# Routed experts behind attention and a dense feed-forward: expert weights split by two engines instead of three, a third early block, and three smaller moves

## Chip, cores and metric

One core of one Trainium2 chip. The metric is device microseconds (us) of one execution; lower is better. Before the change the median of 3 runs is 950.04 us (948.1 to 950.38).

## The reference

Three stages follow one another on 4608 tokens (8 batches of 576) of 512 values.

```python
# attention in chunks of 64, 8 heads of 64
scores = scale * q_c @ k_c.T ; attn = softmax(scores) ; x = attn @ v_c      # 4608 x 512
# dense feed-forward, d_ff 768
h = np.maximum(np.maximum(x @ w1, x @ w2), x @ w3)
x = h @ w_out
# routed experts: only tokens with a positive skip score, one of 8 experts each
do_compute = x @ w_skip > 0
e_idx = np.argmax(xc @ w_gate, axis=1) ; gate_w = softmax(xc @ w_gate)[e_idx]
out[do_compute] = xc + gate_w * (np.maximum(xc @ w1[e], 0) @ w2[e])         # w1 512x1024, w2 1024x512
```

With the inputs that the reference draws, its own routing sends 404, 159, 28, 89, 123, 65, 3 and 85 rows to the experts 0 to 7; of them 318, 105, 21, 70, 109, 25, 0 and 53 come from the first 4096 tokens.

## The kernel before

All stages share one program whose order on every engine is written out by hand, so an instruction that waits holds back all that is behind it on its engine. Every product is made from two halves: a weight or an activation is split into hi (rounded) and lo (the rest), and three matmuls (hi x hi, hi x lo, lo x hi) are summed.

Tokens go through attention and feed-forward in 9 chunks of 512 (`i` = 0 to 8, 8 is `LAST`). While chunk `i` is in the feed-forward, which has 18 slots (6 columns `f` of 128, times 3 weight matrices `m`), attention of the next tokens runs between its matmuls, VectorE makes the routing scores of the chunk before, and chunk `i-2` is placed in the experts' table: `route_pick` in slot 0, `route_place` in slot 2. `route_place` counts with two small matmuls (L532, L533) into a PSUM tile `pos`, which VectorE reads at L537 and L539; `pos` takes its turn in the PSUM ring of the tag "S", from which attention's transposes (`PT`, L279) take theirs too. At a column's end `ff_lo` (L347) makes the lo half of the hidden values on GpSimd, for the very last column on VectorE.

After the last chunk four output tiles are finished (`out_tile`, matmuls at L358). Among them TensorE transposes rows for the routing scores (`logits_turn`, L472, then `logits_pe`, L479) and the rows of two early blocks (`block_x`, L614). `logits_turn(2)` and `block_x` share one PSUM tile, `pxt[0]`.

Then come the experts. A block takes 128 rows of one expert: `block` has 12 matmuls (`first`, L634) for each half of the hidden values, ReLU on ScalarE (L639), four transposes (`turn`, L643) whose hi goes to ScalarE (L645) and lo to VectorE (L646), and 24 matmuls `second` (L651) whose sum VectorE scales by the gate and adds to the rows (L674); GpSimd scatters the rows back to `out` with an indirect DMA (L679). A block's rows come by an indirect DMA from `out` on GpSimd's queue (`gather`, L606), and `block_x` transposes them. Expert 0's first two blocks can start before the routing is complete, since their rows are old ones, of the first 4096 tokens. After them the kernel gathers for all experts from the complete table (`inf_e`, L889; index arithmetic L926 and L927), and every expert has one block whose place is fixed and further blocks behind branches on its count (`chain`, L986).

An expert's weights come in 8 pieces of 512 KB through a ring of 8 raw buffers, loaded on SyncE's queue (`expert_load`, L580 and L584), and `expert_split` makes hi and lo of each while the block of the expert before it runs. Five pieces have hi on ScalarE (L600) and lo on VectorE (L601); the pieces 0, 3 and 6 (for expert 0 two, for expert 1 one) have hi on VectorE (L597) and lo on GpSimd (L598):

```python
if n == 0 or n == 3 and e != 1 or n == 6 and e > 1:
    nc.vector.tensor_copy(hi, t)                                             # L597
    nc.gpsimd.tensor_tensor(out=lo, in0=t, in1=hi.bitcast(F32), op=ALU.subtract)
else:
    nc.scalar.activation(hi, t, AF.Copy)                                     # L600
    nc.vector.tensor_tensor(out=lo, in0=t, in1=hi.bitcast(F32), op=ALU.subtract)
```

## Time and profile before

| | |
|---|---|
| runs, median (lowest to highest) | 950.04 us (948.1 to 950.38) |
| the profiled execution | 951.15 us, its span 949.3 us |
| mean granted TensorE clock | 0.973 of full speed |
| busy: TensorE | 886.6 us, 93% of the span |
| busy: VectorE, ScalarE, GpSimd | 653.4, 286.3, 280.1 us |
| HBM | 80.27 MB read, 12.93 MB written |

The profile names the engines PE (TensorE), PEld (its weight loads), DVE (VectorE), ACT (ScalarE), POOL (GpSimd) and SP (SyncE); a q behind the name is the engine's queue of instructions. Times of single rows count from the start of the span. The routed experts' blocks lie from about 757 to 943 us. The fixed block of expert 1 starts at 821.70, its second at 834.6, then one block each of the experts 2 to 7 begins at 851.2, 866.7, 881.1, 895.3, 910.1 and 928.0. In a timeline row "x4" stands for four instructions in a row, and the bracket tells how long the engine had been idle and what it had waited for.

### The profile page before, as it was taken

The numbers are of one execution on the slowest core, as the hardware profiler recorded it, in microseconds if no ns is written. First come the engines' busy times: TensorE is split into PE (matmuls) and PEld (weight loads), VectorE is DVE, ScalarE is ACT, GpSimd is POOL, SyncE is SP. The second block draws the span as 40 slices with busy tenths as digits, with TensorE's granted clock in tenths as the row PEclk, the third lists the DMA queues.
The fourth block names the chain that finished last, engine by engine and source line by source line (L and its number), as shares of the span: only waits on it lengthen the run. The fifth ranks groups of instructions, "written<-read, shape, count | busy, mean of one in ns | idle before, by whom it ended". The sixth has DMA issues, their size and how long they took to land. (4 is left out here: it accounts for less than half of the span.)

```text
span 949.3 us, 16425 instructions
## 1 busy us (share of the span) xinstructions
PE 886.6 (93%) x6048; PEld 730.0 (77%) x6048; DVE 653.4 (69%) x1374; ACT 286.3 (30%) x468; POOL 280.1 (30%) x204
## 2 busy tenths in 40 slices
PE   7599999999999999999999999999999896989886
PEld 6597778887887887888788788788887775768664
DVE  4668945987777787687787777677582371458983
ACT  4466532112112122112221222221211441335451
POOL 2258841113102111111211211221125132345772
PEclk8799999999999999999999999999999997989999
DMA  7766762224123123212412413100600544146870
GB/s 171 187 161 162 195 196 41 58 49 97 33 51 79 34 37 90 54 30 56 83 30 38 102 32 59 51 7 1 222 1 23 177 129 147 58 157 221 291 258 11
DMA packets 215361, 92.04 MB, mean 97 GB/s; under 512 B 187015, under 2 KB 196487, under 8 KB 215122
## 3 DMA queue, kind: packets, MB, share of 16 engines
q1 hardware_dynamic: 212098, 86.67, 34.7%
q0 software_dynamic: 3152, 3.95, 1.3%
q8 instruction: 63, 1.03, 0.5%
q14 instruction: 48, 0.39, 0.1%
HBM read 80.27 MB, written 12.93 MB: 98 GB/s over the span
## 5 line engine op out<-in xcount | busy, mean ns | idle before, releaser
L331 PE MATMUL A<-arena 128*128 128x512 f32 (+1 forms) x2016 | 471.2, 388 | 1.6 <-POOL arena L404 1.2
L331 PEld LDWEIGHTS A<-arena 128*128 128x128 f32 x2016 | 365.6, 189 | 75.8 <-POOL arena L404 2.6
L466 DVE CUSTOM_DVE_ANT_0 junk<-x,wb 128x512 bf16<-128x512 f32 x270 | 209.6, 776 | 5.9
L347 POOL TENSOR_TENSOR arena<-hs,arena 128x512 fp32r<-128x512 f32 x53 | 80.8, 1524 | 438.4 <-ACT arena L343 438.3
L358 PE MATMUL X<-arena 128*128 128x512 f32 x648 | 158.4, 393 | 1.8 <-POOL arena L347 1.8
L340 DVE TENSOR_TENSOR hs<-A,hs 128x512 f32<-128x512 f32 x108 | 74.2, 687 | 121.4 <-PE A L331 120.5
L358 PEld LDWEIGHTS X<-arena 128*128 128x128 f32 x648 | 122.1, 190 | 27.9 <-POOL arena L347 2.2
L343 ACT ACTIVATE arena<-hs 128x512 fp32r<-128x512 f32 x54 | 34.1, 631 | 239.4 <-DVE hs L340 239.4
L634 PE MATMUL pa<-arena,xT 128*128 128x512 f32 x288 | 79.3, 426 | 7.8 <-PEq L986 3.8
L601 DVE TENSOR_TENSOR arena<-ew,arena 128x1024 fp32r<-128x1024 f32 x43 | 62.7, 1481 | 19.9 <-ACT arena L600 19.9
L634 PEld LDWEIGHTS pa<-arena,xT 128*128 128x128 f32 x288 | 56.4, 203 | 24.3 <-issue 9.1
L651 PE MATMUL py<-arena 128*128 128x512 f32 x288 | 72.0, 397 | 1.4 <-DVE arena L646 1.3
L598 POOL TENSOR_TENSOR arena<-ew,arena 128x1024 fp32r<-128x1024 f32 x21 | 59.5, 2839 | 28.4 <-DVE arena L597 8.8
L651 PEld LDWEIGHTS py<-arena 128*128 128x128 f32 x288 | 53.0, 189 | 14.1 <-DVE arena L646 2.4
L556 POOL DMA_INDIRECT tab<-inf,idx x36 | 39.7, 1103 | 75.6 <-DMA tab<-inf,idx 46.3
L258 DVE TENSOR_REDUCE mx<-S 128x8 f32<-128x512 f32 x36 | 24.8, 690 | 44.5 <-PE S L247 44.5
L338 ACT ACTIVATE hs<-A 128x512 f32<-128x512 f32 x54 | 32.2, 596 | 71.8 <-PE A L331 59.3
L600 ACT ACTIVATE arena<-ew 128x1024 fp32r<-128x1024 f32 x43 | 43.8, 1058 | 21.6 <-DMA ew<-in_moe_w_dram 8.8
L296 PEld LDWEIGHTS O<-PTs,vin 64*64 64x64 f32 x1152 | 38.0, 139 | 14.4 <-issue 10.8
L247 PE MATMUL S<-kT,qT 64*64 64x64 f32 x1152 | 40.8, 222 | 8.6 <-ACT PTs L285 8.3
L296 PE MATMUL O<-PTs,vin 64*64 64x64 f32 x1152 | 42.9, 226 | 2.5 <-ACT PTs L285 2.5
L247 PEld LDWEIGHTS S<-kT,qT 64*64 64x64 f32 x1152 | 37.5, 138 | 10.0 <-ACT PTs L285 8.7
(139 smaller groups left out, 775.7 us busy)
## 6 DMA issues: line engine op xcount, KB each, us to landing
ew<-in_moe_w_dram SPq DMA_DIRECT2D x64, 512.0 KB
vin<-in_v_dram SPq DMA_DIRECT2D x144, 64.0 KB
wst<-in_moe_w_dram SPq DMA_DIRECT2D x18, 512.0 KB
out_dram<-x SPq DMA_DIRECT2D x36, 256.0 KB
qin<-in_q_dram SPq DMA_DIRECT2D x144, 32.0 KB
kin<-in_k_dram SPq DMA_DIRECT2D x144, 32.0 KB
wsto<-in_moe_w_out_dram SPq DMA_DIRECT2D x6, 512.0 KB
wb<-wrow SPq DMA_DIRECT2D x1, 2304.0 KB
```

The lines of the kernel that those rows point to most:

```text
L247: nc.tensor.matmul(ps[64 * j:64 * j + 64, 4 * c + 2 * r + g, :], qt[64 * j:64 * j + 64, p, cols], kt[64 * j:64 * j + 64, p, cols], start=T ...
L296: nc.tensor.matmul(ps[64 * g:64 * g + 64, x, 64 * c:64 * c + 64], vt[64 * g:64 * g + 64, c, x, :], pt[64 * g:64 * g + 64, 2 * c + r, 64 * ...
L331: nc.tensor.matmul(ps[:, ts], a[:, kk, cs], b_[:, kk, ts], start=n == 0, stop=n == 3 * KD - 1)
L340: nc.vector.tensor_tensor(out=hb, in0=ps, in1=hb, op=ALU.max)
L347: eng.tensor_tensor(out=lo, in0=hs[f % 2], in1=hi.bitcast(F32), op=ALU.subtract)
L358: nc.tensor.matmul(X[i, u], a[:, cols], b_[:, f, :], start=(f, n) == (0, 0), stop=(f, n) == (KF - 1, 2))
L466: nc.vector.tensor_tensor_reduce(out=junk, in0=x2[u], in1=wb[:, e, :], scale=1.0, scalar=0.0, op0=ALU.mult, op1=ALU.add, accum_out=lg[i][: ...
L598: nc.gpsimd.tensor_tensor(out=lo, in0=t, in1=hi.bitcast(F32), op=ALU.subtract)
L600: nc.scalar.activation(hi, t, AF.Copy)
L601: nc.vector.tensor_tensor(out=lo, in0=t, in1=hi.bitcast(F32), op=ALU.subtract)
L634: nc.tensor.matmul(pa[n], a[:, kk, :], b_[:, kk, cs], start=a is xhi and b_ is w1h and kk == 0, stop=a is xlo and kk == KD - 1)
L651: nc.tensor.matmul(py, hT[n][m][:, t, :], b_[:, f, :], start=f == 0 and m == 0 and b_ is w2h, stop=f == KF2 - 1 and m == 1)
```

## The change

Five things. (1) Every piece of every expert has hi on ScalarE and lo on VectorE. (2) The first block of expert 1's old rows is added as a third early block: its rows are gathered into `xgs[2]` and transposed inside expert 0's first block in any case; the block runs, in place of expert 1's fixed block, if expert 1 has 128 old rows or more (`n1_old >= P`), and otherwise the program goes on as before. Two branches on `n1_old` and a second register load are new. (3) `pos` takes its turn in the PSUM ring "O" instead of "S", and `logits_turn(2)` writes to `pa4[0]` instead of `pxt[0]`. (4) `ff_lo` of the last chunk's last two columns is VectorE's, before of the last one alone. (5) Expert 0's first scatter is issued ahead of the gathers, the table for the experts 0 and 1 is loaded and turned into indices ahead of that for the others, and the gathers come in another order. The core of the diff:

```diff
 def expert_split(e, n, load=True):
-        if n == 0 or n == 3 and e != 1 or n == 6 and e > 1:
-            nc.vector.tensor_copy(hi, t)
-            nc.gpsimd.tensor_tensor(out=lo, in0=t, in1=hi.bitcast(F32), op=ALU.subtract)
-        else:
-            nc.scalar.activation(hi, t, AF.Copy)
-            nc.vector.tensor_tensor(out=lo, in0=t, in1=hi.bitcast(F32), op=ALU.subtract)
+        nc.scalar.activation(hi, t, AF.Copy)
+        nc.vector.tensor_tensor(out=lo, in0=t, in1=hi.bitcast(F32), op=ALU.subtract)
...
 def logits_turn(u):
-        turn_x((pa4 + pxt)[u], x2[u], lbuf[u])
+        turn_x((pa4[u % 2] if u < 3 else pxt[1]), x2[u], lbuf[u])
 def logits_pe(i, u):
-        logits_mm(i, u, ph[1][:, 0, 0:E + 1] if u == 3 else pa[u % 2][:, 0:E + 1], lbuf[u])
+        logits_mm(i, u, ph[1][:, 0, 0:E + 1] if u == 3 else pa[(u, u, 1)[u]][:, 0:E + 1], lbuf[u])
...
 def route_place(i, u0=0, u1=TPC):
-            ps = psum.tile([P, DM], F32, tag="S", name=f"pos{i}")
+            ps = psum.tile([P, DM], F32, tag="O", name=f"pos{i}")
...
-                    ff_lo(i, f, nc.vector if (i, f) == (LAST, KF - 1) else nc.gpsimd)
+                    ff_lo(i, f, nc.vector if i == LAST and f >= KF - 2 else nc.gpsimd)
...
-                        lbuf = [xgs[1], hs[0], xgs[1], xgs[2]]
+                        lbuf = [xgs[1], hs[0], xgs[1], hs[1]]
...
-                        for j in range(2):
-                            gather(xgs[3 * j], idx_0[:, j:j + 1], LAST * CT)
+                        for j in range(3):
+                            gather(xgs[(0, 3, 2)[j]], idx_0[:, j:j + 1], LAST * CT)
...
         n0_old = nc.values_load(n10[0:1, 0:1], min_val=0, max_val=NTOK)
+        n1_old = nc.values_load(n10[0:1, 1:2], min_val=0, max_val=NTOK)
...
 def finish_routing():
-            nc.sync.dma_start(out=inf_e.rearrange("p e j w -> p e (j w)"),
-                              in_=tabv[:, :, 0:JS, :].rearrange("p e j w -> p e (j w)"))
+            for es in (slice(0, 2), slice(2, E)):
+                nc.sync.dma_start(out=inf_e[:, es].rearrange("p e j w -> p e (j w)"),
+                                  in_=tabv[:, es, 0:JS, :].rearrange("p e j w -> p e (j w)"))
...
             2: [lambda: route_place(LAST, 0, 3)],
+            6: [lambda: block_x(xgs[2], xTs[1])],
...
-        nc.gpsimd.tensor_copy(idx_e, inf_e[:, :, :, 1])
+        scatter()
+        nc.gpsimd.tensor_tensor(out=inf_e[:, 1, 0:1, 1], in0=inf_e[:, 1, 0:1, 1], in1=old[:, 2:3], op=ALU.add)
+        nc.gpsimd.tensor_copy(idx_e[:, 0:2], inf_e[:, 0:2, :, 1])
         fetch(0, 2)
+        fetch(0, 3)
         fetch(1, 0)
         fetch(1, 1)
-        fetch(2, 0)
-        fetch(0, 3)
-        scatter()
+        nc.gpsimd.tensor_copy(idx_e[:, 2:E], inf_e[:, 2:E, :, 1])
...
+        with tc.If(n1_old >= P) as cmp:
+            block(1, xgs[2], xTs[1], ws[0], inf_0[:, 2, 0:1], idx_0[:, 2:3], {7: [lambda: ready(0, 2)]})
+        with cmp.Else():
+            ready(0, 2)
+            ready(1, 0)
+        fetch(2, 0)
...
+                with tc.If(n1_old < P) if e == 1 else nullcontext() as cmp:
+                    block(e, rows_of(e, 0), xT_of(e, 0), ws[0], *gate_idx(e, 0), fill)
+                if e == 1:
+                    with cmp.Else():
+                        for n in range(6):
+                            for step in fill[n]:
+                                step()
+                    for n in range(NPC):
+                        expert_load((e + 1) * NPC + n + NRAW)
```

How the change moves instructions, at three places. First TensorE behind the last chunk, where the third and the fourth output tile are finished (X_3 is the fourth; `pxt` and `pa` are PSUM tiles, `xg` a block's rows, `x_2` and `x_3` output rows). Before:

```order
L479 MATMUL pa_7548<-wnat,hs_103 128x9 x4
L614 MATMUL pxt_7549<-ident,xg_7454 128x128 x4
L472 MATMUL pxt_7549<-ident,x_2_1544 128x128 x4
L358 MATMUL X_3_7660<-arena 128x512 x12
L479 MATMUL pa_7547<-wnat,xg_7452 128x9 x4
L472 MATMUL pxt_7702<-ident,x_3_1545 128x128 x4
L882 TENSOR_LOAD n_7435
```

With the change:

```order
L479 MATMUL pa_7553<-wnat,hs_103 128x9 x4
L610 MATMUL pxt_7554<-ident,xg_7455 128x128 x4
L472 MATMUL pa_7552<-ident,x_2_1544 128x128 x4
L358 MATMUL X_3_7665<-arena 128x512 x12
L479 MATMUL pa_7553<-wnat,xg_7453 128x9 x4
L472 MATMUL pxt_7707<-ident,x_3_1545 128x128 x4
L880 TENSOR_LOAD n_7435
L881 TENSOR_LOAD n_7435
```

The order is the same; the second group of transposes no longer writes to the tile that the first has just filled (`pxt_7549` twice before, `pxt_7554` and `pa_7552` now), and a second register load follows.

Second, GpSimd's queue at the end of expert 0's first block, up to the counts of the experts 0 and 1. Before:

```order
L556 DMA tab<-inf_3_7834,idx_3_7865 36864x2
L598 TENSOR_TENSOR arena<-ew_7574,arena 128x1024
L926 TENSOR_TENSOR inf_e<-inf_e,old 128x2
L927 CAST idx_e<-inf_e 128x32
L606 DMA x_3_1545<-out_dram,idx_e 128x512
L606 DMA xg_7452<-out_dram,idx_e 128x512
L606 DMA x_2_1544<-out_dram,idx_e 128x512
L606 DMA xg_7453<-out_dram,idx_e 128x512
L606 DMA xg_7451<-out_dram,idx_e 128x512
L679 DMA out_dram<-x_0_1542,idx_7458 4608x512
L923 TENSOR_LOAD num x2
```

With the change:

```order
L556 DMA tab<-inf_3_7853,idx_3_7884 36864x2
L675 DMA out_dram<-x_0_1542,idx_7459 4608x512
L928 TENSOR_TENSOR inf_e<-inf_e,old 128x2
L929 TENSOR_TENSOR inf_e<-inf_e,old 128x1
L930 CAST idx_e<-inf_e 128x8
L602 DMA x_3_1545<-out_dram,idx_e 128x512
L602 DMA xg_7452<-out_dram,idx_e 128x512
L602 DMA xg_7453<-out_dram,idx_e 128x512
L602 DMA x_2_1544<-out_dram,idx_e 128x512
L935 CAST idx_e<-inf_e 128x24
L924 TENSOR_LOAD num x2
```

The lo of expert 1's piece 0 has left GpSimd, the scatter stands before the gathers, and the rows of expert 1's fixed block (`xgs[1]`: xg_7452 before, xg_7453 now) are fetched third instead of second.

Third, VectorE in the fixed block of expert 2, whose splits are those of expert 3. Before:

```order
L597 CAST arena<-ew_8463 128x1024
L601 TENSOR_TENSOR arena<-ew_8467,arena 128x1024
L601 TENSOR_TENSOR arena<-ew_8471,arena 128x1024
L597 CAST arena<-ew_8488 128x1024
...
L646 TENSOR_TENSOR arena<-ph_7550,arena 128x512
L601 TENSOR_TENSOR arena<-ew_8535,arena 128x1024
L646 TENSOR_TENSOR arena<-ph_7703,arena 128x512
L616 TENSOR_TENSOR xT_7450<-pxt_7702,xT_7449 128x512
L616 TENSOR_TENSOR xT_7446<-pxt_7549,xT_7445 128x512
L601 TENSOR_TENSOR arena<-ew_8569,arena 128x1024
L597 CAST arena<-ew_8573 128x1024
L601 TENSOR_TENSOR arena<-ew_8577,arena 128x1024
```

With the change:

```order
L597 TENSOR_TENSOR arena<-ew_8697,arena 128x1024
L597 TENSOR_TENSOR arena<-ew_8699,arena 128x1024
L597 TENSOR_TENSOR arena<-ew_8701,arena 128x1024
L597 TENSOR_TENSOR arena<-ew_8703,arena 128x1024
...
L642 TENSOR_TENSOR arena<-ph_7555,arena 128x512
L597 TENSOR_TENSOR arena<-ew_8705,arena 128x1024
L642 TENSOR_TENSOR arena<-ph_7708,arena 128x512
L612 TENSOR_TENSOR xT_7451<-pxt_7707,xT_7450 128x512
L612 TENSOR_TENSOR xT_7447<-pxt_7554,xT_7446 128x512
L597 TENSOR_TENSOR arena<-ew_8707,arena 128x1024
L597 TENSOR_TENSOR arena<-ew_8709,arena 128x1024
L597 TENSOR_TENSOR arena<-ew_8711,arena 128x1024
```

The three casts have become three subtractions, the places are the same; the three casts' work is ScalarE's now, and GpSimd's three subtractions are gone.

## Rows read from the trace of the kernel before

**Rows 1.** Busy time, share of the span and instructions, TensorE.

```profile
PE 886.6 (93%) x6048; PEld 730.0 (77%) x6048; DVE 653.4 (69%) x1374; ACT 286.3 (30%) x468; POOL 280.1 (30%) x204
```

**Rows 2.** Waits of PE, 150 to 733 us: total, times, longest.

```profile
PE PT L279 <- DVE dst L539: 9.5, 6, 1.6
```

**Rows 3.** Timeline of PE at one `route_place`: start, us, instruction, idle before.

```profile
531.50 0.63 PE L279 MATMUL PT<-ident,E 128*128 128x128 f32 x4 [1.59 <-DVE dst L539]
```

**Rows 4.** Timeline of DVE right behind it.

```profile
537.20 0.69 DVE L258 TENSOR_REDUCE mx<-S 128x8 f32<-128x512 f32 x1 [1.75 <-PE S L247]
```

**Rows 5.** Timeline of PE, last chunk and output tiles.

```profile
733.78 0.50 PE L358 MATMUL X<-arena 128*128 128x512 f32 x1 [1.78 <-POOL arena L347]
...
741.93 2.99 PE L358 MATMUL X<-arena 128*128 128x512 f32 x12
...
750.12 0.81 PE L472 MATMUL pxt<-ident,x 128*128 128x128 f32 x4 [2.09 <-DVE xT L616]
750.59 4.53 PE L358 MATMUL X<-arena 128*128 128x512 f32 x12
...
757.18 1.16 PE L634 MATMUL pa<-arena,xT 128*128 128x512 f32 x4 [0.71 <-DVE ms L508]
```

**Rows 6.** Timeline of PE, the experts' blocks.

```profile
790.14 1.11 PE L614 MATMUL pxt<-ident,x 128*128 128x128 f32 x4 [7.08 <-DMA x<-out_dram,idx_e]
...
793.10 6.79 PE L634 MATMUL pa<-arena,xT 128*128 128x512 f32 x18 [0.73 <-ACTq L989]
...
821.70 1.64 PE L634 MATMUL pa<-arena,xT 128*128 128x512 f32 x6 [0.53 <-PEq L986]
...
851.20 1.22 PE L634 MATMUL pa<-arena,xT 128*128 128x512 f32 x2 [3.30 <-PEq L986]
```

**Rows 7.** Timeline of POOL around the first gathers from the complete table.

```profile
780.55 0.46 POOL L926 TENSOR_TENSOR inf_e<-inf_e,old 128x2 f32<-128x2 f32 x1 [3.66 <-DMA inf_e<-tab]
...
782.12 1.50 POOL L606 DMA_INDIRECT x<-out_dram,idx_e  x1 [0.83 <-ACT arena L600]
783.92 1.02 POOL L606 DMA_INDIRECT xg<-out_dram,idx_e  x1 [0.30 <-issue]
```

**Rows 8.** The line of the gathers (L606), 690 us to the end.

```profile
DMA to landing us min/median/max: 2.2/6.5/8.8
```

**Rows 9.** A stretch: us, busy PE, PEld, DVE, ACT, POOL, clock, DMA share, GB/s.

```profile
783.10:790.20 7.10, 0.06 (x1) 0.06 (x1) 1.38 (x2) 0.00 (x0) 4.54 (x5) 0.85 1.00 344
```

**Rows 10.** Stretches, block by block: the same columns.

```profile
821.70:834.60 12.90, 12.90 (x64) 10.75 (x65) 11.58 (x11) 7.82 (x11) 8.59 (x4) 1.00 0.50 165
...
851.20:866.70 15.50, 15.40 (x64) 12.33 (x64) 11.43 (x12) 7.91 (x11) 5.83 (x5) 0.84 0.57 193
866.70:881.10 14.40, 13.62 (x64) 10.54 (x64) 14.16 (x12) 8.22 (x11) 12.08 (x5) 1.00 0.69 217
...
910.10:928.00 17.90, 14.86 (x64) 11.66 (x64) 14.75 (x13) 8.21 (x11) 12.11 (x6) 0.90 0.68 249
```

**Rows 11.** Groups by line, 821.7 to 941.7: busy, mean ns, idle before.

```profile
L601 DVE TENSOR_TENSOR arena<-ew,arena 128x1024 fp32r<-128x1024 f32 x30 | 47.4, 1594 | 5.6 <-ACT arena L600 5.5
L600 ACT ACTIVATE arena<-ew 128x1024 fp32r<-128x1024 f32 x30 | 30.8, 1061 | 21.3 <-DMA ew<-in_moe_w_dram 8.8 <-PEq L986 6.7 <-PE pa L634 5.7
L646 DVE TENSOR_TENSOR arena<-ph,arena 128x512 fp32r<-128x512 f32 x16 | 11.0, 685 | 14.0 <-ACT arena L645 13.8
L616 DVE TENSOR_TENSOR xT<-pxt,xT 128x512 fp32r<-128x512 f32 x14 | 9.0, 678 | 4.1 <-ACTq L986 4.1
L674 DVE SCALAR_TENSOR_TENSOR x<-py,inf_e,xg 128x512 f32<-128x512 f32 x8 | 5.9, 741 | 4.5 <-PE py L651 4.5
```

**Rows 12.** Timeline of DVE, two splits.

```profile
835.50 1.21 DVE L601 TENSOR_TENSOR arena<-ew,arena 128x1024 fp32r<-128x1024 f32 x1
...
876.10 3.04 DVE L601 TENSOR_TENSOR arena<-ew,arena 128x1024 fp32r<-128x1024 f32 x1
```

**Rows 13.** Timeline of POOL beside the second of them.

```profile
875.66 2.40 POOL L598 TENSOR_TENSOR arena<-ew,arena 128x1024 fp32r<-128x1024 f32 x1 [0.63 <-DVE arena L597]
```

43 lines of the change are left out of this document (23 added, 20 removed).

## Prediction

> **What bounds the kernel now.** I began with the busy shares: TensorE is busy 93% of the span, 886.6 of 949.3 us [rows 1], so the other 62.7 us are all that can be won without touching its work, and only places where TensorE waits, or runs at a lower clock, count. Then I read TensorE's waits. In the chunks one wait repeats: `PT` waits for VectorE's L539, 9.5 us in 6 times [rows 2]. Then its timelines, the last chunk and the output tiles [rows 5] and the experts' blocks [rows 6], where the brackets show each pause and its releaser. Last, the experts' phase cut into blocks [rows 10]: the reader is to see that TensorE needs 12.9 us for a block (821.70: busy 12.90 of 12.90), that the blocks from 866.70 on take 14.4 to 17.9, and that VectorE is then busy nearly without a break (14.16 of 14.40) while TensorE is not. The bound is TensorE in the chunks and VectorE in the later expert blocks.
>
> **The PSUM ring (3).** At one `route_place` the transposes had to wait 1.59 us until VectorE had read `pos` with L539 [rows 3]: both take tiles from ring "S". With `pos` in ring "O" this order is gone: six chunks, **-9.5** [rows 2]. What is late next: attention's scores, then the max on VectorE. That max found VectorE idle for 1.75 us [rows 4], so VectorE has room for scores that come 1.6 us earlier. "O" is read out by attention's outputs; if its tile came late, the two counting matmuls would stand before the same transposes again, a gain of 0 at worst. I take the whole, since the wait is the same in all six.
>
> **Last chunk and output tiles (3, 4).** With the lo of column 4 on VectorE, TensorE no longer waits 1.78 us for GpSimd's L347, which stood behind the two early gathers in GpSimd's queue: -1.8 [rows 5]. GpSimd's third gather falls into the same place and holds back only table work. The transposes that waited 2.09 us until VectorE had read `pxt` now write to another tile: -2.1 [rows 5]. Right behind that pause 12 matmuls took 4.53 us, where 12 of the same kind took 2.99 before it, so 1.5 us went to a lower clock after the pause; without the pause I take it to stay away: -1.5 (bounds 0 and -1.5). The second register load: the nearest row is the first block's start, 0.71 idle with a load ahead of it [rows 5]; bounds 0 and 0.7, I take 0.3. Sum **-5.1**.
>
> **The third early block (2).** The routing worked out on the reference's inputs leaves expert 1 with 105 old rows. 105 is under 128, so the block is not run: the branch goes to the way of before, and the fixed block of expert 1 stays. What remains of it are costs. Its rows' four transposes take 0.6 us of TensorE (as the four in [rows 3], 0.63): **+0.6**. ScalarE's and VectorE's share of it, 0.6 and 0.7 us, lies beside the block's matmuls. Two branches more: one falls into the pause for the gathers and costs nothing there; one stands before expert 1's fixed block. Such a jump left TensorE idle for 0.53 us at one place and 3.30 at another [rows 6]. I take **+0.7** in all, near the small end, since the code that is jumped to follows closely; the ends are 0 and 5.6 (3.30 and 2.3 at the low clock behind it, as below).
>
> **The gathers (5).** TensorE stood still for 7.08 us until the rows of expert 0's third block landed, and the next 18 matmuls took 6.79 us where full speed (2.99 for 12) makes 4.5 [rows 5, 6]: 2.3 us more at a low clock. The first gather was issued at 782.12, its rows landed at 790.14, 8.0 us later [rows 6, 7]; the line's median is 6.5, its range 2.2 to 8.8 [rows 8]. In that stretch the DMA engines were busy throughout, share 1.00 at 344 GB/s [rows 9]; the expert loads fill them. GpSimd had waited for `inf_e` until 780.55, then two short operations, then 0.83 [rows 7]. The change asks for a quarter of the table first, and GpSimd is rid of a split; against that stand a scatter ahead of the gathers, which must land first, and one operation more. Expert 1's rows come third in the queue instead of second, one issue later (1.3 to 1.8 us by the starts in [rows 7]), and both transposes stand before the next block. I take **-1.0**, with the ends +2 (the place in the queue alone) and -9.4 (pause and slow matmuls gone). The slow matmuls stay in my sum.
>
> The Trainium skill, "DMA: Bandwidth & Descriptors", section SWDGE vs HWDGE vs iDMA, says that GpSimd's DMAs and SyncE's feed different queues of each DMA engine, between which it takes turns: by it the gathers share with the loads instead of standing behind them, a landing moves with its issue, and the term is -1.0; if they stood behind all loads issued before, an earlier issue would bring nothing, and the term would be 0. No row here decides between the two, since the share was 1.00 in that stretch [rows 9].
>
> **The splits (1).** From 866.70 to 928.00 four blocks with splits take 61.3 us [rows 10]. VectorE's subtraction takes 1.21 us by itself, and 3.04 when GpSimd's of 2.40 us runs beside it [rows 12, 13]; its mean over these blocks is 1.594 [rows 11]. So the two hinder each other, and the GpSimd splits also return raw buffers late. With the change VectorE has per block 8 subtractions of 1.21, 2 of `turn` at 0.685, 2 of `block_x` at 0.678 and one scaling at 0.741 [rows 11, 12]: 9.68 + 1.37 + 1.36 + 0.74 = 13.15 us. ScalarE gets 8 casts at 1.06 [rows 11] in place of 5: 8.2 + 3.2 = 11.4 [rows 10]. TensorE needs 12.9. The longest is 13.15; I take 13.3 for the small waits between three engines that are all nearly full, so 4 x 13.3 = 53.2 instead of 61.3: **-8.1**. The ends are 12.9 a block (-9.7) and 14.4 a block (-3.7). The block at 851.20 stays at 15.5, since it has the slow clock (0.84) behind the jump of 3.30 [rows 6, 10]. The fixed block of expert 1 is TensorE's already, and 13.15 against 12.9 is hidden by the jump block behind it, which has no splits of its own.
>
> **The sum.** -9.5 - 5.1 + 0.6 + 0.7 - 1.0 - 8.1 = -22.4. The profiled execution took 951.15 us (span 949.3), so 928.75; it lies 1.11 above the median of the runs, 950.04, so I forecast **927.6** for the median.
>
> **The rivals.**
>
> *As forecast*, 927.6: chance 0.60.
>
> *VectorE stays the bound at the old period.* It is busy 14.16 of 14.40 now [rows 10], and its share of the splits grows from 5 subtractions and 3 casts to 8 subtractions. If the 13.15 is stretched by waits for ScalarE, which now makes every hi first, blocks stay near 14.4: 4 x 1.1 = 4.4 more, 932.0. For it: ScalarE's 11.4 leave little room, and VectorE had waited 5.5 us for its casts [rows 11]. Against it: GpSimd, the cause of the long rows, is gone. 0.17.
>
> *The rows land in time.* If the smaller table and the earlier issue let expert 0's and 1's rows land before TensorE needs them, the rest of the pause (6.1) and the slow matmuls (2.3) go too: 919.2. Against it: a landing took 6.5 us in the median, and the scatter comes first. 0.08.
>
> *The third block does run.* If 128 old rows or more go to expert 1, it fills that pause: about 919 as well. Against it: the count, 105. 0.02.
>
> *New jumps at the dear price.* If the jump over the new code costs what the one at 851.20 did, 3.30 and the slow clock behind it 2.3, then 4.9 comes on top of the 0.7: 932.5. The rows do not tell why one jump cost 0.53 and another 3.30 [rows 6]. 0.10. The Trainium skill, "Runtime: NRT & Kernel Launch", section Instruction fetch mechanics, says that instructions are fetched ahead in sequence, in blocks of 16 KiB, and that a taken branch to a place outside the fetched window stalls the engine until it is fetched. Two prices for the same kind of jump agree with it; by that rule the new branches pay whenever a whole block of code is jumped over, which is what the case `n1_old < P` does once for the early block.
>
> *Slower: the splits starve the blocks.* If VectorE's long rows come not from GpSimd but from something that stays (the loads, ScalarE's writes), 8 subtractions a block instead of 5 make it worse. From 1.92 us a subtraction on, the five blocks from 851.20 take (8 x 1.92 + 3.47) x 5 = 94 us instead of 76.8, which eats all other gains and ends 0.3% above before. At the mean of the two rows, 2.13, it is 102.5 us, hence 927.6 + 8.1 + 25.7 = 961.4. Against it: the long row has GpSimd's beside it, the short one has not [rows 12, 13]. 0.03.
>
> **The numbers.** About 0.3%, 2.9 us, is what a measurement of this kernel can tell from no change. Every case but the last is faster by more than that: 0.97, of which I leave 0.02 for several mishaps at once that end near no change; so faster 0.95, same 0.02, slower 0.03. The range goes from 918 (rows landed in time, or the third block) to 937 (old period and dear jump together, 936.9). That leaves out the last rival and combinations beyond.
>
> **What would show it.** Right: no wait of `PT` for L539; no pause near 733 and 750, and 12 matmuls there in 3.0 us; a pause of about 6 us before the third block; subtractions of 1.2 us everywhere; blocks from expert 3's on of 13.1 to 13.5 us; both branches on `n1_old` taken the old way. Wrong: blocks still over 14 us, a new pause of 3 us at expert 1's fixed block, `PT` waiting for another reader, or subtractions that stay over 1.5 us without GpSimd.

## The result, and the profile after

The changed kernel takes 925.23 us (median of 4 runs, 924.17 to 927.86); the kernel before, on the same chip, 949.47 (now 4 runs). The ratio is 0.975 with a 95% interval of 0.9724 to 0.9776: faster. The forecast was 927.6, range 918 to 937. The profiled execution after took 924.21 us (span 922.4), the one before 951.15 (949.3), so the two traces differ by 26.9 us in the span, the medians by 24.2. One run of the kernel e10_hold5 below, 985.22 us at a granted clock of 0.841, is a slow one and is left out of its median.

The page after, engines as in [rows 1]: TensorE has 10.8 us less of busy time and is 95% busy, GpSimd 60 us less.

```profile
PE 875.8 (95%) x6052; PEld 723.4 (78%) x6052; DVE 644.5 (70%) x1377; ACT 306.2 (33%) x490; POOL 220.2 (24%) x185
```

The list of TensorE's waits from 150 to 730 us, one row before [rows 2], is empty after. TensorE's timeline, to be held against [rows 5, 6] (x36: the first output tiles; L610 are the transposes of `block_x`, L630 the `first` matmuls):

```profile
717.66 8.32 PE L358 MATMUL X<-arena 128*128 128x512 f32 x36
...
735.15 3.00 PE L358 MATMUL X<-arena 128*128 128x512 f32 x12
...
740.75 3.04 PE L630 MATMUL pa<-arena,xT 128*128 128x512 f32 x12 [1.25 <-DVE gs L514]
...
773.54 1.09 PE L610 MATMUL pxt<-ident,x 128*128 128x128 f32 x4 [6.86 <-DMA x<-out_dram,idx_e]
775.53 1.09 PE L610 MATMUL pxt<-ident,xg 128*128 128x128 f32 x4 [0.91 <-DMA xg<-out_dram,idx_e]
777.40 6.01 PE L630 MATMUL pa<-arena,xT 128*128 128x512 f32 x18 [0.78 <-ACTq L1007]
...
806.19 4.45 PE L630 MATMUL pa<-arena,xT 128*128 128x512 f32 x18 [1.46 <-ACT arena L596]
...
832.51 4.47 PE L630 MATMUL pa<-arena,xT 128*128 128x512 f32 x18 [0.73 <-ACTq L1004]
...
847.40 4.44 PE L630 MATMUL pa<-arena,xT 128*128 128x512 f32 x18 [1.78 <-PEq L1004]
```

The pauses at 733 and 750 are gone, and the 12 matmuls take 3.00 us. The pause for the gathers is not shorter but longer: 6.86 and 0.91 where [rows 6] have 7.08. The 18 matmuls behind it still run at a low clock: the granted clock is 0.50, the lower of its two levels (1.2 GHz), from 773.50 to 777.40, and 0.70 in the mean from there to 783.20. The jump to expert 2's block costs 0.73 instead of 3.30, and no slow matmuls follow. Expert 1's fixed block starts after a pause of 1.46 where it was 0.53. The blocks, as in [rows 10], and the two groups that share the splits, as in [rows 11]:

```profile
832.50:847.40 14.90, 13.11 (x65) 10.63 (x65) 13.31 (x15) 11.07 (x15) 2.60 (x2) 1.00 0.69 220
847.40:860.60 13.20, 13.06 (x64) 10.58 (x65) 10.97 (x12) 11.03 (x15) 2.06 (x2) 1.00 0.89 316
860.60:874.60 14.00, 13.04 (x64) 10.57 (x65) 13.31 (x15) 11.06 (x15) 3.10 (x2) 1.00 0.94 323
```

```profile
L597 DVE TENSOR_TENSOR arena<-ew,arena 128x1024 fp32r<-128x1024 f32 x48 | 56.3, 1221 | 9.7 <-ACT arena L596 8.0 <-DVEq L1004 0.9 <-SPq L1004 0.4
...
L596 ACT ACTIVATE arena<-ew 128x1024 fp32r<-128x1024 f32 x47 | 47.2, 1057 | 3.4 <-PEq L1004 3.1 <-ACTq L1004 0.3
```

VectorE's subtraction takes 1.221 us in the mean, 1.594 before, and TensorE is now busy in a block for all but the jump. In the four blocks from 847.40 to 901.02 TensorE is busy 52.20 of 53.62 us, VectorE 48.49. Where the time went, cut at starts of TensorE's rows (us; each figure is the difference of two starts; the first stretch begins at the same transposes of the second chunk, 141.75 before and 141.08 after):

| stretch | before | after | difference | forecast |
|---|---|---|---|---|
| chunks and output tiles, to the first block | 615.43 | 599.67 | -15.8 | -14.6 |
| expert 0's first block | 13.45 | 13.51 | +0.1 | +0.6 |
| its second block and the pause | 22.47 | 23.14 | +0.7 | -1.0 |
| from its third block to expert 2's | 58.10 | 55.11 | -3.0 | +0.7 |
| blocks of the experts 2 to 6 | 76.86 | 68.51 | -8.4 | -8.1 |

What is missing to 26.9 lies ahead of the first stretch (-0.7) and behind the last (+0.1).

### The profile page after: what moved, and what is told of

It is laid out like the page before. It is cut to its first block, busy times and chain, and to the rows that moved or that the text cites. A ratio compares the mean times of both kernels' runs of the same rounds, so it can differ in the third digit from the quotient of the medians.

```text
span 922.4 us, 16467 instructions
## 1 busy us (share of the span) xinstructions
PE 875.8 (95%) x6052; PEld 723.4 (78%) x6052; DVE 644.5 (70%) x1377; ACT 306.2 (33%) x490; POOL 220.2 (24%) x185
## 5 line engine op out<-in xcount | busy, mean ns | idle before, releaser
L597 DVE TENSOR_TENSOR arena<-ew,arena 128x1024 fp32r<-128x1024 f32 x64 | 75.1, 1221 | 21.2 <-ACT arena L596 19.5
L630 PE MATMUL pa<-arena,xT 128*128 128x512 f32 x288 | 74.7, 408 | 8.1 <-PEq L1004 2.7
L630 PEld LDWEIGHTS pa<-arena,xT 128*128 128x128 f32 x288 | 53.4, 192 | 22.7 <-ACTq L1004 4.0
L596 ACT ACTIVATE arena<-ew 128x1024 fp32r<-128x1024 f32 x64 | 64.0, 1056 | 7.5 <-PEq L1004 6.3
L556 POOL DMA_INDIRECT tab<-inf,idx x36 | 40.3, 1119 | 81.7 <-DMA tab<-inf,idx 46.4
L247 PE MATMUL S<-kT,qT 64*64 64x64 f32 x1152 | 40.5, 222 | 6.5 <-ACT PTs L285 6.3
L247 PEld LDWEIGHTS S<-kT,qT 64*64 64x64 f32 x1152 | 37.2, 138 | 7.9 <-ACT PTs L285 6.6
L265 ACT ACTIVATE E<-E 128x512 f32<-128x512 f32 x36 | 22.8, 632 | 54.6 <-DVE E L260 54.6
```

Of the source, the lines that this page charges most:

```text
L247: nc.tensor.matmul(ps[64 * j:64 * j + 64, 4 * c + 2 * r + g, :], qt[64 * j:64 * j + 64, p, cols], kt[64 * j:64 * j + 64, p, cols], start=T ...
L556: nc.gpsimd.indirect_dma_start(out=tab[:, :], out_offset=bass.IndirectOffsetOnAxis(ap=idx[:, u:u + 1], axis=0), in_=inf[:, u, :], in_offse ...
L630: nc.tensor.matmul(pa[n], a[:, kk, :], b_[:, kk, cs], start=a is xhi and b_ is w1h and kk == 0, stop=a is xlo and kk == KD - 1)
```

## The experiments

Twelve kernels. In each paragraph the time is the median and the ratio that to the kernel before on the same chip; kernels of different comparisons are compared by their ratios and by lengths of stretches within a trace.

**e1_splits: part 1 alone.**

```diff
-        if n == 0 or n == 3 and e != 1 or n == 6 and e > 1:
-            nc.vector.tensor_copy(hi, t)
-            nc.gpsimd.tensor_tensor(out=lo, in0=t, in1=hi.bitcast(F32), op=ALU.subtract)
-        else:
-            nc.scalar.activation(hi, t, AF.Copy)
-            nc.vector.tensor_tensor(out=lo, in0=t, in1=hi.bitcast(F32), op=ALU.subtract)
+        nc.scalar.activation(hi, t, AF.Copy)
+        nc.vector.tensor_tensor(out=lo, in0=t, in1=hi.bitcast(F32), op=ALU.subtract)
```

> The kernel before with part 1 alone: every expert piece has hi on ScalarE and lo on VectorE. Theory (GpSimd's subtractions lengthen VectorE's beside them): VectorE's subtractions fall from a mean of 1.594 to about 1.22 us in the expert blocks, the four blocks from expert 3's on go from 61.3 to about 53.2 us, and the whole to 941.4 (8.1 less). If the pause before expert 2's block, 3.30 us before and 0.73 in the changed kernel, also comes from part 1, another 2.6 to 3.3 goes: about 938.5. Rival (VectorE stays full, waits for ScalarE's hi take the place): blocks stay at 14.4, 946.

935.58 us, ratio 0.9875 (0.9837 to 0.9912). The five blocks take 68.12 us instead of 76.86, VectorE's subtractions 1.222. The jump to expert 2's block costs 1.65, with no slow matmuls behind it, so the gain there comes with part 1. One thing nobody expected: the second block and its pause shrink from 22.47 to 18.76.

```profile
776.60 1.82 POOL L602 DMA_INDIRECT x<-out_dram,idx_e  x1 [0.83 <-PE py L647]
```

```profile
784.21 0.66 PE L610 MATMUL pxt<-ident,x 128*128 128x128 f32 x4 [3.46 <-DMA x<-out_dram,idx_e]
...
843.14 4.46 PE L630 MATMUL pa<-arena,xT 128*128 128x512 f32 x18 [1.65 <-PEq L982]
```

These are GpSimd's and TensorE's timelines of e1_splits: the first gather goes out 8.3 us after the start of expert 0's second block (768.31), before it was 11.5 (782.12 against 770.63), and the pause is 3.46 and not 7.08. So this trace has a gain of some 4 us here that the changed kernel's has not. Part 5 looks like the reason; what all the runs show of that is put together under the gathers below.

**e2_pos: `pos` in the other ring alone.**

```diff
-            ps = psum.tile([P, DM], F32, tag="S", name=f"pos{i}")
+            ps = psum.tile([P, DM], F32, tag="O", name=f"pos{i}")
```

> The kernel before with the counting tile pos in ring O alone. Theory: all six waits of PT for L539 go and nothing takes their place; the shift per chunk is the 1.73 us that the changed kernel shows at its six steps (10.4 in all), 939.3. Rival (the step is the 1.59 that the wait shows, the rest is from elsewhere): 9.5, 940.0; the six steps of the PT starts tell these apart (1.73 or 1.59 each). Second rival (scores or attention's outputs become late): a wait of S or O of over 0.5 us at each chunk and less than 5 us gained.

936.1 us, ratio 0.9871 (0.983 to 0.9911). The wait of `PT` is gone in all six chunks and none has taken its place. The step from one `PT` row to the next across a `route_place` is 24.53 us (193.62 to 218.15), before 26.28 (193.38 to 219.66): 1.75 a chunk, 10.5 by the starts of all six, not the 9.5 of the wait alone. The interval of the ratio is too wide to tell the two apart; the rows do. This kernel still has the pause for `pxt`, but not the slow matmuls behind it, and it keeps the dear jump:

```profile
739.42 0.66 PE L472 MATMUL pxt<-ident,x 128*128 128x128 f32 x4 [2.09 <-DVE xT L616]
739.83 3.00 PE L358 MATMUL X<-arena 128*128 128x512 f32 x12
...
838.68 6.81 PE L634 MATMUL pa<-arena,xT 128*128 128x512 f32 x18 [3.26 <-PEq L986]
```

**e3_tiles: the other PSUM tile and column 4's lo alone.**

```diff
-        turn_x((pa4 + pxt)[u], x2[u], lbuf[u])
+        turn_x((pa4[u % 2] if u < 3 else pxt[1]), x2[u], lbuf[u])
...
-                    ff_lo(i, f, nc.vector if (i, f) == (LAST, KF - 1) else nc.gpsimd)
+                    ff_lo(i, f, nc.vector if i == LAST and f >= KF - 2 else nc.gpsimd)
```

> The kernel before with the third token tile's transposes in another PSUM tile and the lo of the last chunk's column 4 on VectorE. Theory: both pauses (1.78 and 2.09) and the slow matmuls behind the second (1.5) go: 5.4 less, 944.2, and the first expert block starts about 5.4 earlier. Rival (the slow clock comes anyway, from the transposes): 3.9 less, 12 matmuls at 4.5 us again, 945.6.

941.38 us, ratio 0.9932 (0.9907 to 0.9956). From the start of the output tiles to the first block it takes 22.6 us (727.23 to 749.84), before 28.5 (728.66 to 757.18): 5.9 less, both pauses and the slow matmuls:

```profile
744.72 3.00 PE L358 MATMUL X<-arena 128*128 128x512 f32 x12
```

The theory holds, with its condition: in e2_pos the slow matmuls stayed away although the pause was there, so 1.5 of this term is not the pause's own price every time.

**e4_noblock: the change without the third early block.** In short:

```diff
-                        for j in range(3):
+                        for j in range(2):
...
-        n1_old = nc.values_load(n10[0:1, 1:2], min_val=0, max_val=NTOK)
...
-            6: [lambda: block_x(xgs[2], xTs[1])],
...
-        with tc.If(n1_old >= P) as cmp:
-            block(1, xgs[2], xTs[1], ws[0], inf_0[:, 2, 0:1], idx_0[:, 2:3], {7: [lambda: ready(0, 2)]})
-        with cmp.Else():
-            ready(0, 2)
-            ready(1, 0)
+        ready(0, 2)
+        ready(1, 0)
```

> The changed kernel without the third early block: no third gather, no transposes of its rows, no second register load, no branches on expert 1's old rows. Theory (the block is dead weight): 0.6 for the transposes, 0.3 for the register load and 0.7 for the branches: 923.6, 1.6 less than the changed kernel. Rival (the place of the code decides what a jump costs): the pauses before the blocks of experts 1, 2, 3 and 5 (1.46, 0.73, 1.78, 0.97 us) move by up to 3 us in either direction, and the whole ends between 921 and 929. Second rival (the third gather holds back what follows on GpSimd): the landing of expert 0's third block moves by more than 1 us.

923.2 us, ratio 0.974 (0.9695 to 0.9786), the changed kernel 0.975: no difference that can be told. By stretches: the first block 13.41 (13.51 with it), from the third block to expert 2's 55.68 (55.11), the blocks from there 66.97 (68.51). Expert 1's fixed block starts after a pause of 1.31, so the 1.46 after the change is not its branch's. This kernel keeps one move that came with part 2: the count and the branch hint for the next expert stand ahead of that block, where they stood inside it. The pause is 0.42 to 0.53 in the four kernels without this move (the kernel before, e1_splits, e2_pos, e3_tiles) and 1.31 to 1.57 in every kernel with it that runs the block; no run undoes it alone. Small jump pauses do move (1.49 before expert 2's block, 0.22 before expert 3's), as the rival has it, but by up to 1.6 us, not 3. Over the four stretches the third block's code costs about 0.9, all of it in the last, where only such pauses differ. The sign of the second rival is there, but without a price: the rows of expert 0's third block are awaited until 17.13 us after the start of the second block instead of 19.28, those of expert 1 until 21.41 (21.27), and TensorE needs both (23.22 and 23.14 for the stretch).

**e5_hold: the loads held.**

```diff
-            expert_split(1, 0)
+            expert_split(1, 0, False)
...
-            5: splits(1, range(1, 4))}, hold=True)
+            5: splits(1, range(1, 4), False)}, hold=True)
...
-        for n in range(4, NPC):
-            expert_load(NPC + n + NRAW)
+        for n in range(NPC):
+            expert_load(NPC + n + NRAW, True)   # True: nc.vector.memset(t[:, 0:1], 0.0) ahead of the load
```

> The changed kernel with the eight 512 KB loads of expert 2's pieces held until the rows of expert 0's third block have landed (VectorE writes one column of each raw tile behind that block's subtraction, the load waits for it). Theory (the loads fill the DMA engines, so the table and the gathers land late): the table lands about 2.5 us after its issue instead of 4.3, the gathers 2.2 to 3 instead of 7.8, TensorE's pause before the third block shrinks from 6.9 + 0.9 to about 2, and with the shorter pause the 18 matmuls behind it take 4.5 instead of 6.0: 6 to 7.5 less than the changed kernel, about 918.5. Rival (the gathers' own chain from table to landing sets the pause): the pause stays over 5, 924 to 925. If the held loads come too late for expert 2's splits, ScalarE waits for ew in expert 1's blocks, and the gain is given back there.

923.01 us, ratio 0.9707 (0.9672 to 0.9742), an interval that overlaps the changed kernel's. The line of the gathers, 760 to 775 us, in the changed kernel and then in e5_hold:

```profile
DMA to landing us min/median/max: 6.5/6.7/7.6
```

```profile
DMA to landing us min/median/max: 2.8/3.1/3.4
```

With the loads away a landing takes less than half the time. The pause shrinks to 3.40 and 0.40, not to 2, the 18 matmuls take 6.54, and the stretch is 18.70 us instead of 23.14. GpSimd's timeline shows what is late now:

```profile
763.82 0.97 POOL L679 DMA_INDIRECT out_dram<-x,idx  x1 [1.83 <-DVE x L674]
...
769.36 1.07 POOL L606 DMA_INDIRECT x<-out_dram,idx_e  x1 [3.77 <-ACT arena L600]
```

The indices are there at 765.6 (the end of the cast L934), the gather goes out 3.8 us later. ScalarE's L600 is the releaser that the row names, but the scatter fits better: it landed 4.7 us after 763.82, at 768.5, and 0.84 later the gather starts, the same 0.84 that lies between the indices and the first gather in e9_undo5 and e10_hold5, where the scatter stands behind. So in this trace, where the indices are early, the scatter ahead of the gathers (part 5) sets the start. In the changed kernel it doesn't: there the scatter landed 5.2 us after 759.25, at 764.45, and the indices were ready only at 765.02.

**e6_beside: GpSimd's work put back, read by nobody.**

```diff
+        if e > 2 and n in (0, 3, 6):
+            hv = hi.bitcast(F32)
+            for h_ in range(2):
+                half = hv[:, h_ * DM:(h_ + 1) * DM] if n < KD else hv[:, h_, :]
+                nc.gpsimd.tensor_tensor(out=beside[0], in0=beside[0], in1=half, op=ALU.subtract)
```

> The changed kernel with GpSimd work put back beside: for the pieces 0, 3 and 6 of the experts 3 to 7, GpSimd subtracts that piece's hi from a scratch tile, two instructions of 128 x 512, read by nobody; the raw buffers do not wait for it. The output is the reference's. Theory (VectorE's subtractions were long because GpSimd's ran beside them): VectorE's mean goes up from 1.22 to 1.5 us or more in the blocks of the experts 2 to 6, these blocks go from 13.2-14.9 back to 14.2 or more, total 928 to 932. Rival (late returned raw buffers or VectorE's casts made the blocks long): VectorE's subtractions stay at 1.22 and the time at 925.

944.38 us, ratio 0.9943 (0.9917 to 0.9969), the changed kernel 0.975: some 18 of the 24 us are gone. Its groups in the blocks of the experts 2 to 6 (838 to 922 us), and one of its blocks:

```profile
L598 DVE TENSOR_TENSOR arena<-ew,arena 128x1024 fp32r<-128x1024 f32 x38 | 67.9, 1836 | 1.6 <-DVEq L1011 1.2 <-SPq L1011 0.4
...
L603 POOL TENSOR_TENSOR x<-x,arena 128x512 f32<-128x512 f32 x30 | 58.2, 1938 | 2.8 <-DVE arena L598 0.8
```

```profile
869.90:888.80 18.90, 15.10 (x64) 11.72 (x65) 18.68 (x15) 11.06 (x14) 16.29 (x9) 0.91 0.74 251
```

Nothing but GpSimd's instructions was added, they hold no raw buffer back, and VectorE's subtractions go from 1.221 to 1.836 us; VectorE is busy 18.68 of 18.90. The five blocks take 83.62. This is the decisive run for part 1: beside GpSimd's subtractions VectorE's take longer, and on a VectorE that is full this is paid in full. The direction was expected, the size was not (928 to 932). It is dearer than before (76.86). VectorE has 8 subtractions a block here and had 5, and GpSimd works for longer (58.2 us in these blocks, 52.3 from 821.7 to 941.7 before); no run tells these two apart.

The trace of the kernel before shows what the lengthening looks like. In [rows 12, 13] GpSimd's subtraction ends at 878.06, and VectorE's, begun in between, ends 1.08 us later. The other way round, where GpSimd's starts second:

```profile
882.60 1.21 DVE L601 TENSOR_TENSOR arena<-ew,arena 128x1024 fp32r<-128x1024 f32 x1
```

```profile
882.82 3.25 POOL L598 TENSOR_TENSOR arena<-ew,arena 128x1024 fp32r<-128x1024 f32 x1 [2.75 <-DVE arena L597]
```

VectorE's ends at 883.81, GpSimd's 2.26 later, and the shortest of GpSimd's takes 2.37. In both pairs the one that starts second ends about its own length after the first: they look as if they took turns.

**e7_runs: the third block does run.**

```diff
-                            old[:, 2:3], cnt[:, 0, 1:2], float(NTOK + P), BIG, op0=ALU.is_ge, op1=ALU.mult)
+                            old[:, 2:3], cnt[:, 0, 1:2], float(NTOK + P // 2), BIG, op0=ALU.is_ge, op1=ALU.mult)
...
-        with tc.If(n1_old >= P) as cmp:
+        with tc.If(n1_old >= P // 2) as cmp:
...
-                with tc.If(n1_old < P) if e == 1 else nullcontext() as cmp:
+                with tc.If(n1_old < P // 2) if e == 1 else nullcontext() as cmp:
```

> The changed kernel with the condition for the third early block at 64 old rows instead of 128, so that with expert 1's 105 old rows it does run; expert 1's old rows beyond the 105 up to 128, that is its new rows 105 to 127, are left out. Theory (the block fills the pause for the gathers): TensorE's pause before expert 0's third block (7.8 us in the changed kernel) and the slow matmuls behind it (1.5) go, the fixed block of expert 1 is not run: about 9 less, 916. Rival (the splits of expert 2, which lay beside the fixed block, now hold up expert 1's second block on VectorE, 8 times 1.22 us): up to 5 us of that is given back, 921.

921.27 us, ratio 0.9714 (0.9682 to 0.9747), an interval that overlaps the changed kernel's. Since it leaves out 23 of expert 1's rows, this kernel is a probe and no replacement. Both theory and rival are in the rows:

```profile
770.96 4.36 PE L630 MATMUL pa<-arena,xT 128*128 128x512 f32 x18
...
784.35 4.47 PE L630 MATMUL pa<-arena,xT 128*128 128x512 f32 x18 [0.73 <-ACTq L1007]
...
811.90 0.63 PE L610 MATMUL pxt<-ident,x 128*128 128x128 f32 x4 [1.78 <-DVEq L1004]
...
815.68 6.01 PE L630 MATMUL pa<-arena,xT 128*128 128x512 f32 x18 [2.72 <-ACT xT L611]
```

The block of old rows runs at 770.96, the third block of expert 0 follows without a pause or a low clock; but where expert 1's fixed block was, its second now stands behind ScalarE and VectorE with the splits of expert 2, 1.78 and 2.72 of pause, and 1.5 of slow matmuls. From the second block to expert 2's it takes 72.0 us (758.70 to 830.72) instead of 78.25: 6.2 gained, of 9 expected.

**e8_order: expert 1's rows second in the queue.**

```diff
         fetch(0, 2)
-        fetch(0, 3)
         fetch(1, 0)
         fetch(1, 1)
+        fetch(0, 3)
```

> The changed kernel with expert 1's rows gathered second instead of third, all else kept. Theory (the third place in the queue costs one issue, 1.3 us): the second transposes behind the pause no longer wait (0.91 us in the changed kernel) and the block starts about 1 us earlier, 924.2. Rival (landings do not follow the issues): no change.

927.31 us, ratio 0.9764 (0.9727 to 0.9801): no difference in the time that can be told, and not the 924.2 of the theory. In the trace the second transposes no longer wait, and the stretch is 22.34 us, 0.8 less: that is the price of the third place in the queue, and it is too small for the medians.

**e9_undo5: part 5 undone** (expert 1's rows second in the queue, as in e8_order).

```diff
-        scatter()
         nc.gpsimd.tensor_tensor(out=inf_e[:, 0, 0:2, 1], in0=inf_e[:, 0, 0:2, 1], in1=old[:, 0:2], op=ALU.add)
...
-        nc.gpsimd.tensor_copy(idx_e[:, 0:2], inf_e[:, 0:2, :, 1])
+        nc.gpsimd.tensor_copy(idx_e, inf_e[:, :, :, 1])
...
+        scatter()
-        nc.gpsimd.tensor_copy(idx_e[:, 2:E], inf_e[:, 2:E, :, 1])
```

> The changed kernel with part 5 undone: the table loaded and turned into indices in one piece, the first scatter behind the gathers, expert 1's rows second in the queue. The kernel of before with part 1 alone reached its third block 18.8 us after the start of the second, the changed kernel 23.1. Theory (part 5 costs what part 1 gave there): about 19 us again, 921 in all, 4 less than the changed kernel. Rival (the difference is how the loads happen to meet the table and the gathers): still 22 to 23 us, 925.

925.47 us, ratio 0.9729 (0.9688 to 0.9769). The first gather goes out 8.4 us after the start of the second block (763.92 against 755.55), as in e1_splits, in the changed kernel 11.5 (765.76 against 754.26), 3 us later. But the landing takes 7.0 to 7.9 us under the loads, the second transposes wait 2.18 for theirs, and the stretch is 21.09, half way. Between 925 and 921 this run doesn't decide. Nor does it show that part 5 makes the 3 us: in e11_best and e12_fill part 5 is undone too, and the first gather goes out at 11.5 again.

**e10_hold5 and e11_best: loads held and part 5 undone; then without the third block too.** Their edits are those of e5_hold, e9_undo5 and e4_noblock.

> The changed kernel with part 5 undone (scatter behind the gathers) and the eight loads held until the rows have landed. With the loads held alone, table and gathers landed in 2 to 3 us but the first gather was issued 3.8 us after its indices were there, 0.8 after expert 0's scatter had landed. Theory (with the loads away, the scatter ahead of the gathers is what sets the pause): first gather at about 764 to 765, its rows 2.8 us later, before TensorE gets to them at 768; pause under 2 us, no slow matmuls behind it; 8 to 9 less than the changed kernel, 917. Rival (something else holds the first gather back): the pause stays at 3 us or more, 921 to 923.

> The same without the third early block (no third gather, no transposes for it, no branches on expert 1's old rows). Theory (dead weight on these inputs): 1 to 2 less than with it, 915.5. Rival (the place of the code moves the jumps' prices): within 2 us of it in either direction.

e10_hold5: 922.32 us, ratio 0.9728 (0.9697 to 0.9758). The second block and its pause take 17.09 us instead of 23.14, 6.0 less, but in the time little of that is seen: the interval overlaps the changed kernel's, and 917 was expected. The first gather goes out at 765.27, as the theory has it. The waits left are 0.3 and 2.09, and still the matmuls behind them are slow:

```profile
772.13 1.09 PE L614 MATMUL pxt<-ident,xg 128*128 128x128 f32 x4 [2.09 <-DMA xg<-out_dram,idx_e]
774.00 6.60 PE L634 MATMUL pa<-arena,xT 128*128 128x512 f32 x18 [0.78 <-ACTq L1009]
```

e11_best: 919.2 us, ratio 0.9685 (0.965 to 0.9719), the fastest kernel here and the only one that is faster than the changed kernel by an interval clear of its own, if barely (0.9719 against 0.9724). Expected was 915.5. Its stretches are 18.49 (second block and pause), 56.54 and 67.03, in all as long as those of e10_hold5 (17.09, 56.27 and 68.86), so the traces don't show what the third block's code costs here.

**e12_fill: matmuls in the pause.**

```diff
+        idle_mm(11)      # nc.tensor.matmul(pa[0], a0[:, 0, :], b0[:, 0, 0:512], start=True, stop=True)
         ready(0, 2)
+        idle_mm(3)
         ready(1, 0)
+        idle_mm(3)
```

> The last kernel (no third block, part 5 undone, loads held) with 17 matmuls that compute nothing used, in the pause before expert 0's third block: 11 before the first transposes, 3 between the two, 3 behind them, each 0.25 us, so that TensorE does not stand still there. Theory (the low clock behind the pause comes from TensorE standing still): the 18 matmuls of the third block take 4.5 instead of 6.3 us, and the kernel is 1.5 to 2 faster than the last one, 917.4. Rival (the clock falls there for another reason): 6.3 again, and the 17 matmuls cost up to 1 us where the rows have already landed: 919 to 920.

921.19 us, ratio 0.9713 (0.9685 to 0.9741). TensorE's timeline:

```profile
768.92 2.73 PE L951 MATMUL pa<-arena,xT 128*128 128x512 f32 x11
772.08 0.63 PE L614 MATMUL pxt<-ident,x 128*128 128x128 f32 x4 [0.43 <-DMA x<-out_dram,idx_e]
...
775.22 4.45 PE L634 MATMUL pa<-arena,xT 128*128 128x512 f32 x18 [0.32 <-PEq L1006]
```

The 18 matmuls take 4.45 us at a granted clock of 1.00 (775.22 to 779.60), where e11_best has 6.30 at 0.67 (774.48 to 780.70): the low clock here comes from TensorE standing still. From the second block to expert 0's fourth it takes 32.0 us (756.64 to 788.64), in e11_best 33.75 (755.99 to 789.74). In the median the 1.75 us don't show; the two ratios' intervals overlap.

## Why the prediction was right, point by point

**The PSUM ring**, -9.5: right in mechanism, 10.5 in size. The wait's bracket counts from the modelled end of the matmul before to the start of the transposes (1.59); the shift of the following rows is 1.75 by e2_pos.

**Last chunk and output tiles**, -5.1: -5.4 in the trace (728.66 to 757.18 before, 717.66 to 740.75 after), 5.9 alone in e3_tiles. The second register load was put at 0.3; the pause before the first block grew by 0.5 (0.71 to 1.25). Over all the kernels with the load it is 0.84 to 1.25, without it 0.43 to 0.83, so the size fits. What I took for certain and is not, is that slow matmuls belong to the pause (e2_pos).

**The third block**, +0.6 and +0.7: it isn't run, as counted. The transposes are there, but the first block is only 0.1 longer: from their start to the next block's they hold TensorE for 0.35 us (753.91 to 754.26), since the row's 0.60 overlaps what follows, and before TensorE stood still for some 0.3 at this place. The branches cost nothing that can be found: the stretch has 55.11 with them and 55.68 without.

**The gathers**, -1.0: a step of this sum that failed, +0.7 in the trace. I expected the smaller table and the missing GpSimd split to send the first gather earlier. It goes out 11.50 us after the start of the second block, before it was 11.49. The rows of expert 0's third block are there 0.2 earlier (19.28 and 19.51), and the third place in the queue costs 0.9 (the wait for expert 1's rows; e8_order has it gone), which makes the +0.7. So the place in the queue was weighed about rightly (1.3 to 1.8 by the rows), and the gain set against it did not come.

Why not? I took part 5 for the cause, since the first gather is 3 us earlier in e1_splits and e9_undo5, which lack it. All traces together speak against that. The table has every kernel that doesn't run the third early block, in us. Its second column tells by how much GpSimd's third write of the routing table (L556) starts after VectorE's first split of expert 1, the third how long that write takes; the first gather counts from the start of the second block, and the stretch is the second block and its pause.

| kernel | third write after VectorE's split | its length | part 5 | loads held | first gather | stretch |
|---|---|---|---|---|---|---|
| e1_splits | -0.01 | 0.97 | no | no | 8.29 | 18.76 |
| e9_undo5 | -0.12 | 0.97 | no | no | 8.37 | 21.09 |
| e10_hold5 | -0.12 | 0.97 | no | yes | 8.36 | 17.09 |
| e5_hold | -0.12 | 0.97 | yes | yes | 10.57 | 18.70 |
| before | 0.07 | 1.47 | no | no | 11.49 | 22.47 |
| e2_pos | 0.10 | 1.44 | no | no | 11.47 | 22.21 |
| e3_tiles | 0.03 | 1.50 | no | no | 11.47 | 22.83 |
| changed | 0.13 | 1.94 | yes | no | 11.50 | 23.14 |
| e4_noblock | 0.05 | 2.01 | yes | no | 10.64 | 23.22 |
| e6_beside | 0.30 | 1.77 | yes | no | 11.50 | 23.48 |
| e8_order | 0.07 | 2.00 | yes | no | 11.50 | 22.34 |
| e11_best | 0.44 | 1.63 | no | yes | 11.47 | 18.49 |
| e12_fill | 0.33 | 1.74 | no | yes | 11.47 | 18.58 |

The early gathers go with a third write that starts just ahead of VectorE's splits, the late ones with a write that starts just behind them, with part 5 or without. The two sides in rows, first the changed kernel, then e9_undo5 (VectorE's row, then GpSimd's):

```profile
753.08 4.63 DVE L597 TENSOR_TENSOR arena<-ew,arena 128x1024 fp32r<-128x1024 f32 x4
```

```profile
753.21 1.94 POOL L556 DMA_INDIRECT tab<-inf,idx  x1 [1.37 <-DMA tab<-inf,idx]
...
764.01 0.61 POOL L928 TENSOR_TENSOR inf_e<-inf_e,old 128x2 f32<-128x2 f32 x1 [3.79 <-DMA inf_e<-tab]
...
765.76 1.48 POOL L602 DMA_INDIRECT x<-out_dram,idx_e  x1 [0.74 <-ACT arena L596]
```

```profile
754.42 4.62 DVE L597 TENSOR_TENSOR arena<-ew,arena 128x1024 fp32r<-128x1024 f32 x4
```

```profile
754.30 0.97 POOL L556 DMA_INDIRECT tab<-inf,idx  x1 [1.37 <-DMA tab<-inf,idx]
...
763.92 1.74 POOL L602 DMA_INDIRECT x<-out_dram,idx_e  x1 [0.84 <-ACT arena L596]
```

Behind a long third write the fourth is late as well, and then the table and its indices. A shift of some 0.1 us between two engines thus goes with 3 us at the gather. No run moves the write alone, so that the lengthened write is the cause is likely but not shown. What is shown of part 5 is less than I thought: where the indices are early and the loads are held, the scatter ahead keeps the first gather until 10.57 (e5_hold), without it 8.36 (e10_hold5). In the changed kernel the indices are the later of the two. The landings, 6.5 to 7.6 us there, are long because of the loads (2.8 to 3.4 in e5_hold), and the four kernels with the loads held have 17.1 to 18.7 us in that stretch, the others 18.8 to 23.5.

The question that I left open, whether the gathers share with the loads or stand behind all that were issued before, is not settled by the shorter landings, which both would give. A gather that goes out 3 us earlier lands 3 us earlier (e9_undo5: its rows are awaited until 16.30 instead of 19.28), though the four loads issued ahead of it, the same in both kernels, are only 1.4 us earlier there (5.06 and 6.43 us after the start of the second block): it doesn't just end with them. That fits what the Trainium skill, "DMA: Bandwidth & Descriptors", section SWDGE vs HWDGE vs iDMA, says of queues between which an engine takes turns.

**The splits**, -8.1: -8.4 for the five blocks, by another composition. The block of expert 2 was left at 15.5 and came to 14.89, without the slow clock but with a jump of 1.78 behind it; the next are 13.21, 14.01, 13.21 and 13.19, mean 13.4, where 13.3 was taken. One of the four lies outside the 13.1 to 13.5 that the text gave as a sign, the 14.01 with a jump of 0.97 behind it. That GpSimd's subtractions made the blocks long is shown by e6_beside and not only argued. The limit that the text named is another one: it added up 13.15 us of VectorE a block, but VectorE's rows overlap a little (two subtractions take 2.36, not 2.44), it is busy 12.1 us a block in the mean (48.49 in four), and TensorE, busy 13.05, sets the pace. That 13.3 fits so well is in part luck. And the 1.594 of [rows 11] is the mean from 821.7 to 941.7, not that of the four blocks alone.

**What the sum lacked**, -3.0: the dear jump before expert 2's block. The stretch to its start is 3.2 shorter there, 0.8 shorter by the less slow matmuls of the third block (6.01, before 6.79) and 0.9 longer at expert 1's fixed block. The text kept 3.30 and the slow matmuls, for want of a reason why it should change. This is the other step that failed, a term put at nothing. e1_splits has 1.65 and full speed there, e2_pos and e3_tiles 3.26 and 3.11 with 6.8 for the 18 matmuls, so part 1 alone takes the most of it. The ten other kernels with part 1 have 0.73 to 2.02 there. How is open: in the three kernels with the long pause, packets of the two instruction queues lie within it (one or two of each kind), in e1_splits and in the changed kernel one. The Trainium skill, "Runtime: NRT & Kernel Launch", section Instruction fetch mechanics, would have a stall there for code that isn't fetched yet; these packets fit it. That no jump in the changed kernel costs over 1.78, with more code to jump over than before, speaks against the rival that I built on it, and no run moved code alone.

In the trace the sum was 4.5 short, 22.4 against 26.9: most of it the stretch with the jump (3.7, of which 0.7 had been set aside for branches) and the ring (1.0), against 1.7 too much for the gathers. In the medians it is 1.8, since the profiled run before lay 1.7 above its median here and the one after 1.0 below its own. So the ring, the tiles and the splits were forecast rightly, and that the whole came so close is in part luck: an unforeseen gain at the jump made up for the gathers. The rival of a saturated VectorE is out: it is busy 11.0 to 13.3 us of a block, ScalarE 11.1. The slower case hung on subtractions of 1.92 us and they take 1.22; e6_beside, at 1.84, shows how near that price is once GpSimd works beside, even though its five blocks take 83.62 us and not 94.

## What to carry to other kernels

Work moved to an idle GpSimd is not free if VectorE is full: price it by VectorE's rows while GpSimd runs, not by GpSimd's own. Where a pause ends with a gather, try holding back bulk loads that nobody needs yet: here its landing went from 6.5 to 7.6 us to 2.8 to 3.4, though of the 4.4 to 6.0 us that the stretch gained only part showed in the medians. When a pause can't be closed, look at what follows it: in e10_hold5 waits of 2.4 us cost another 2.1 in clock. And before a difference between two traces is put down to an edit, look for it in all the traces there are: two runs seemed to lay 3 us to part 5, and two others without part 5 speak against it.

## What was not expected

Pauses of the same length are not followed by the low clock every time: after 2.09 us of standing still, 12 matmuls took 4.53 us before and 4.58 in e1_splits, but 3.00 in e2_pos (granted clocks 0.63, 0.62 and 1.00); after 1.25 and 1.02 us ahead of the first block they took 3.04 in the changed kernel (1.00) and 4.58 in e5_hold (0.62), whose instructions up to there are the same. And traces of the same instructions differ between comparisons: one row of each chunk's scores (L247, 32 matmuls) takes 1.10 us in the changed kernel and 1.39 to 1.50 in e7_runs, 2.0 us over five chunks (381.20 and 383.18 between the same two rows), so that stretches, not whole spans, were compared here.
